# Decode step of two layers: in each pair's step the maximum's product and the exponential ahead of the preceding pair's value products; the kept pair's query product and output weights early

## The chip, the cores and the metric

One core of one Trainium2 chip. The metric is the device time of one launch in microseconds (us). The kernel before takes 515.19 us, the median of 3 runs (514.79 to 515.29). In the profiles PE is TensorE (matrix products), DVE VectorE, ACT ScalarE, POOL GpSimd, and SP the engine that issues the loads from HBM, the large memory, into SBUF, the core's own.

## The reference, cut to what matters

```python
x = x + A(layernorm(x)); x = x + B(layernorm(x))        # twice
def A(x, k_cache, v_cache, wq, wo):                     # B=Sq=1, D=640, 32 heads, Dh=192
    q = (x @ wq) per head
    k, v = the last W=4096 rows of the caches of each head
    p = softmax(q.k * Dh**-0.5);  o = p @ v
    return o.reshape(1, 1, 32*192) @ wo
def B(x, w_gate, w_up, w_down):                         # F=1536
    return (sigmoid(x @ w_gate) * (x @ w_up)) @ w_down
```

One token, bfloat16, the same weights and caches in both layers. In each layer every cache row is used for one product, so the work per byte is tiny. 219 MB pass from HBM into SBUF.

## The kernel before

The 32 heads go in 16 pairs. A pair has an A part (query weights and keys, 3.64 MB, in an A slot) and a B part (values and output weights, 3.64 MB, in a B slot). Layer one loads pair p's A part and pair p-1's B part in one transfer of 7.27 MB ("c" in `seq`, the order of the one DMA queue). A transfer is issued when both slots are free: `QK` frees an A slot, `PVn` (the output product) frees a B slot. Some pairs stay in SBUF for layer two; the "kept pair" PM = 1 keeps only its A part, and its output weights ("wom") are loaded over its query weights once its layer-two query product is done.

```python
    seq = [("a", 0, 0)] + [("c", 0, p) for p in range(1, 15)] + [("a", 0, 15), ("b", 0, 14)] + last_values(0, 15)
    seq += [("wol", 14), ("wol", 15)] + [(k,) for k in (*MW, *MV)] + [("a0", 0), ("a0", 1), ("a0", 2), ("a", 1, 3), ("b", 1, 2)]
    seq += [("wom",), ("b", 1, 3), ("a", 1, 4), ...]
    # [cut]
    def soft(x=0, hook=None, mid=None):
        # DVE: maximum of each score row
        pg.op("dve", lambda v: v.reduce_max(out=mx, in_=sc_x[0][:], axis=AX.X), ...)
        # ACT: diag = identity * maximum
        pg.op("act", lambda a: a.mul(out=diag[:], in_=ident, mul=mx), ...)
        if mid is not None:
            mid()
        # PE: the product that spreads the maximum over all partitions; DVE: two small ops make the bias
        pg.op("pe", lambda t: t.matmul(dmx[:, 0:P], lhsT=ones_f, rhs=diag[:], ...), ..., ex=[rb[2]])
        # [cut]
    def expo(x=0): ...   # ACT: e = exp(scores*s + bias), with its sum
    def ET(z): ...       # PE: 8 products transpose e; DVE copies it to et_sb
    def PVmm(p, z): ...  # PE: 32 value products; ACT: 2 evictions (o8_sb)
    def PVt(z): ...      # PE: RS, the sums' product (bank 4), and the transpose of o8; DVE: oTb = o * 1/sum
    def PVn(p, z): ...   # PE: 15 output products into yT, then release(slot of the values)

    def step(p, prev):
        if l == 0 and prev > 0:
            PVn(prev - 1, 1 - prev % 2)
        Q(p, 0)
        QK(p, 0)
        soft(0, mid=lambda: PVmm(prev, prev % 2))
        PVt(prev % 2)
        if l == 1:
            PVn(prev, prev % 2)
        expo()
        ET(p % 2)
```

Each engine runs its operations in program order, so the order of these calls is the order on PE, DVE and ACT. `step` runs 25 times: 15 in layer one, 10 in layer two.

## Time and profile before

| | |
|---|---|
| time | 515.19 us |
| busy | PE 49%, DVE 19%, ACT 17% |
| DMA | 218.97 MB, mean 426 GB/s; the main queue busy 99.2% of 16 engines' span |

The page of the kernel before; each digit after DMA is the busy share of a fortieth of the span in tenths, q1 is the main DMA queue with its share of 16 engines' span, and the last line is the chain of waits by engine:

```profile
span 513.6 us, 8566 instructions
DMA  9999999999999999999999999999999999999996
DMA packets 9676, 218.97 MB, mean 426 GB/s; under 512 B 1208, under 2 KB 1208, under 8 KB 4664
q1 hardware_dynamic: 9512, 218.63, 99.2%
DMA 66%; PE 22%; DVE 5%; ACT 3%; SPq 2%; issue 2%; DVEq 0%; POOL 0%; ACTq 0%; POOLq 0%
```

The queue has no hole of the size of a slice: DMA is the limit from end to end. The packets say it more sharply: a packet of 56,832 B takes 2,098 ns, which for 16 engines is 433 GB/s. The Trainium skill (DMA: Bandwidth & Descriptors, section "Where 436 GB/s comes from") gives 435.2 GB/s as the ceiling of the fabric; this trace agrees to 0.4%.

### The profile page before, as it was taken

The numbers are of one execution on the slowest core, as the hardware profiler recorded it, in microseconds if no ns is written. First come the engines' busy times: TensorE is split into PE (matmuls) and PEld (weight loads), VectorE is DVE, ScalarE is ACT, GpSimd is POOL, SyncE is SP. The second block draws the span as 40 slices with busy tenths as digits, with TensorE's granted clock in tenths as the row PEclk, the third lists the DMA queues.
The fourth block names the chain that finished last, engine by engine and source line by source line (L and its number), as shares of the span: only waits on it lengthen the run. The fifth ranks groups of instructions, "written<-read, shape, count | busy, mean of one in ns | idle before, by whom it ended". The sixth has DMA issues, their size and how long they took to land.

```text
span 513.6 us, 8566 instructions
## 1 busy us (share of the span) xinstructions
PE 250.7 (49%) x3716; PEld 136.8 (27%) x3716; DVE 97.8 (19%) x376; ACT 84.9 (17%) x171; POOL 4.3 (1%) x31
## 2 busy tenths in 40 slices
PE   0463255424543255325656767774535424543665
PEld 0231122112221122112325434442212112321234
DVE  0221212111210121112221333231212111210311
ACT  0110111011110111011121024130211011101220
POOL 0010000000000000000000000000000000000000
PEclk9965666566766666566665558686656566655765
DMA  9999999999999999999999999999999999999996
GB/s 425 429 422 425 426 431 438 456 434 425 429 425 434 430 438 451 438 429 425 410 417 408 407 440 429 424 432 429 446 430 447 434 443 429 425 430 423 423 429 286
DMA packets 9676, 218.97 MB, mean 426 GB/s; under 512 B 1208, under 2 KB 1208, under 8 KB 4664
## 3 DMA queue, kind: packets, MB, share of 16 engines
q1 hardware_dynamic: 9512, 218.63, 99.2%
q8 instruction: 13, 0.21, 0.1%
q10 hardware_dynamic: 144, 0.06, 0.0%
q14 instruction: 7, 0.06, 0.0%
HBM read 218.69 MB, written 0.00 MB: 426 GB/s over the span
## 4 chain that ended last, share of the span: by engine, by line
DMA 66%; PE 22%; DVE 5%; ACT 3%; SPq 2%; issue 2%; DVEq 0%; POOL 0%; ACTq 0%; POOLq 0%
DMA big<-in_uc_dram 57%; PE scores L409 8%; PE o L466 7%; DMA big<-in_wd_dram 6%; DMA big<-in_wu_dram 3%; ACT e_sb L433 3%; SPq L212 2%; PE bank L394 2%; PE bank L425 2%; PE bank L500 1%; DVE sc L426 1%; PE bank L439 1%; DVE qs L397 1%; DVE sc L419 1%; DVE sc L428 1%
## 5 line engine op out<-in xcount | busy, mean ns | idle before, releaser
L394 PE MATMUL bank<-sh,big 128*128 128x1 bf16 x480 | 17.7, 166 | 163.3 <-DMA big<-in_uc_dram 160.5
L409 PE MATMUL scores<-big,qs 128*32 128x512 bf16 x744 | 83.3, 617 | 10.3 <-DVE qs L397 10.3
L466 PE MATMUL o<-big,et_sb 128*2 128x384 bf16 x1024 | 76.8, 468 | 13.4 <-POOL sc L248 11.6
L422 ACT ACTIVATE diag<-cst,sc 128x128 f32<-128x128 bf16 x32 | 12.9, 402 | 326.7 <-PE o L466 210.6
L394 PEld LDWEIGHTS bank<-sh,big 128*128 128x128 bf16 x480 | 15.2, 104 | 167.4 <-issue 162.1
L419 DVE TENSOR_REDUCE sc<-scores 128x1 f32<-128x1024 f32 x31 | 37.9, 1223 | 78.9 <-PE scores L409 78.9
L466 PEld LDWEIGHTS o<-big,et_sb 128*2 128x2 bf16 x1024 | 32.1, 116 | 59.7 <-issue 39.8
L397 DVE TENSOR_TENSOR qs<-bank,cst 128x96 bf16<-128x96 f32 x32 | 8.2, 257 | 180.8 <-PE bank L394 180.8
L433 ACT ACTIVATE e_sb<-scores,sc 128x1024 bf16<-128x1024 f32 x31 | 37.3, 1204 | 20.3 <-DVE sc L428 18.0
L409 PEld LDWEIGHTS scores<-big,qs 128*32 128x32 bf16 x744 | 24.1, 134 | 44.6 <-issue 32.1
L473 ACT CAST o_sb<-o 128x384 bf16<-128x384 f32 x64 | 29.3, 472 | 25.9 <-PE o L466 25.5
L439 PE MATMUL bank<-cst,e_sb 128*128 128x8 bf16 x256 | 11.5, 168 | 25.6 <-ACT e_sb L433 25.4
L500 PE MATMUL bank<-sh,big 128*128 128x1 bf16 x480 | 17.0, 164 | 10.3 <-DVE sh L489 8.8
L426 DVE TENSOR_REDUCE sc<-bank 128x2 f32<-128x128 f32 x32 | 9.3, 292 | 60.3 <-PE bank L425 60.3
L425 PE MATMUL bank<-diag,sc 128*128 128x128 f32 x64 | 17.8, 364 | 4.8 <-ACT diag L422 4.6
L500 PEld LDWEIGHTS bank<-sh,big 128*128 128x128 bf16 x480 | 14.5, 98 | 12.9 <-DVE sh L489 8.8
L425 PEld LDWEIGHTS bank<-diag,sc 128*128 128x128 f32 x64 | 11.2, 219 | 19.7 <-ACT o_sb L473 9.6
L439 PEld LDWEIGHTS bank<-cst,e_sb 128*128 128x128 bf16 x256 | 8.7, 98 | 29.0 <-DVE sh L489 19.2
L443 DVE CAST et_sb<-bank 128x64 bf16<-128x64 f32 x32 | 7.2, 224 | 41.5 <-PE bank L439 41.5
L486 PE MATMUL bank<-cst,o_sb 128*128 128x1 bf16 x192 | 10.0, 167 | 7.0 <-DVE sc L426 6.2
L451 DVE RECIPROCAL sc<-o 64x1 f32<-64x1 f32 x64 | 10.5, 164 | 10.9 <-PE o L449 9.9
L449 PEld LDWEIGHTS o<-sc 128*128 128x128 f32 x64 | 10.7, 209 | 2.4 <-ACT o_sb L473 1.5
(70 smaller groups left out, 104.3 us busy)
## 6 DMA issues: line engine op xcount, KB each, us to landing
big<-in_uc_dram SPq DMA_DIRECT2D x20, 7104.0 KB, 24.6
big<-in_uc_dram SPq DMA_DIRECT2D x12, 3552.0 KB, 20.9
big<-in_uc_dram SPq DMA_DIRECT2D x1, 3072.0 KB, 22.8
big<-in_uc_dram SPq DMA_DIRECT2D x4, 768.0 KB, 13.6
big<-in_uc_dram SPq DMA_DIRECT2D x5, 480.0 KB, 13.5
big<-in_uc_dram SPq DMA_DIRECT2D x1, 2048.0 KB, 10.6
big<-in_uc_dram SPq DMA_DIRECT2D x1, 2016.0 KB, 13.0
big<-in_wg_dram SPq DMA_DIRECT2D x4, 480.0 KB, 15.8
```

The lines of the kernel that those rows point to most:

```text
L394: ins = t.matmul(qe[:, i:i + 1], lhsT=slot(sa, c * 2 * DH + c0, P), rhs=xq[:, c:c + 1], start=(c == 0), stop=(c == DC - 1))
L397: pg.op("dve", lambda v: v.tensor_tensor(out=qs[:, y], in0=qe[:, 0:3].unsqueeze(2).to_broadcast([P, 3, 32]), in1=mask3, op=ALU.mult), rd=[ ...
L409: ins = t.matmul(sc_x[1 + b][32 * j:32 * j + 32, :], lhsT=qs[:, y, k, :], rhs=slot(sa, WQE + k * W + (4 * b + j) * 512, 512), start=(k == ...
L419: pg.op("dve", lambda v: v.reduce_max(out=mx, in_=sc_x[0][:], axis=AX.X), wr=[res("mx")], ex=sc_x[3:5])
L422: pg.op("act", lambda a: a.mul(out=diag[:], in_=ident, mul=mx), rd=[res("cst"), res("mx")], wr=[res("diag")])
L425: pg.op("pe", lambda t: t.matmul(dmx[:, 0:P], lhsT=ones_f, rhs=diag[:], start=True, stop=True), rd=[res("diag"), res("ones")], ex=[rb[2]])
L426: pg.op("dve", lambda v: v.tensor_reduce(out=nb2, in_=dmx[:, 0:P].rearrange("p (a r) -> p r a", r=2), axis=AX.X, op=ALU.max, negate=True), ...
L433: pg.op("act", lambda a: a.activation(out=e_sb[:], in_=sc_x[0][:], func=ACT.Exp, bias=nbias, scale=srs_c, accum_out=rowsum), rd=[res("nbia ...
L439: ins = t.matmul(qe[:, 0:2 * NB].rearrange("p (r x) -> p r x", r=2)[:, :, 4 * b:4 * b + 4], lhsT=e_sb[:, b * P:(b + 1) * P], rhs=sel, star ...
L466: ins = t.matmul(o8[h][32 * j:32 * j + 2, 0:2 * DH].rearrange("p (a d) -> p a d", a=2), lhsT=et_sb[:, z, h * NB + 2 * u:h * NB + 2 * u + 2 ...
L473: pg.op("act", lambda a, h=h: a.copy(out=o8_sb[:, :, h * DH:(h + 1) * DH], in_=o8[h][:, 0:2 * DH].rearrange("p (a d) -> p a d", a=2)), wr= ...
L500: ins = t.matmul(yT[:, j:j + 1], lhsT=wo[:, c * D + j * P:c * D + (j + 1) * P], rhs=oTb[z][:, c:c + 1], start=False, stop=(c == 2), skip_g ...
```

## The change

Its intent: shorten the chain of a step (scores, maximum, spread product, exponential) by letting it no longer wait for the value products of the preceding pair; have the output weights of the kept pair in the queue earlier, where the queue is thin; and shorten the end of layer one. No byte and no operation goes away.

```diff
-    seq += [...] + [("a0", 0), ("a0", 1), ("a0", 2), ("a", 1, 3), ("b", 1, 2)]
-    seq += [("wom",), ("b", 1, 3), ...]
+    seq += [...] + [("a0", 0), ("wom",), ("a0", 1), ("a0", 2), ("a", 1, 3), ("b", 1, 2)]
+    seq += [("b", 1, 3), ...]
@@ step
             QK(p, 0)
-            soft(0, mid=lambda: PVmm(prev, prev % 2))
+            soft(0)
+            expo()
+            PVmm(prev, prev % 2)
+            ET(p % 2)
             PVt(prev % 2)
             if l == 1:
                 PVn(prev, prev % 2)
-            expo()
-            ET(p % 2)
@@ end of layer one (RS and Q get a parameter for their bank; PVt can leave RS out)
             PVmm(p, 1)
+            RS(1, 2)
             PVn(p - 1, 0)
-            PVt(1)
+            PVt(1, False)
             PVn(p, 1)
@@ layer two, start
             mark("a14_0", Q(14, 0))
+            mark("QM", Q(PM, 1, 5))
[cut]
             QK(0, 0)
-            mark("QM", Q(PM, 1))
             soft(0, mid=lambda: PVmm(14, 0))
```

More of the change, by code (lines that the diff above doesn't have):

```diff
@@ L227, in decode_kernel @@
     seq = [("a", 0, 0)] + [("c", 0, p) for p in range(1, 15)] + [("a", 0, 15), ("b", 0, 14)] + last_values(0, 15)
-    seq += [("wol", 14), ("wol", 15)] + [(k,) for k in (*MW, *MV)] + [("a0", 0), ("a0", 1), ("a0", 2), ("a", 1, 3), ("b", 1, 2)]
-    seq += [("wom",), ("b", 1, 3), ("a", 1, 4), ("b", 1, 4), ("a", 1, 5), ("a", 1, 6), ("b", 1, 5)]
+    seq += [("wol", 14), ("wol", 15)] + [(k,) for k in (*MW, *MV)] + [("a0", 0), ("wom",), ("a0", 1), ("a0", 2), ("a", 1, 3), ("b", 1, 2)]
+    seq += [("b", 1, 3), ("a", 1, 4), ("b", 1, 4), ("a", 1, 5), ("a", 1, 6), ("b", 1, 5)]
     seq += [("c", 1, p) for p in range(7, 13)] + [("a", 1, 13), ("b", 1, 12)] + last_values(1, 13)
@@ L386, in attention, with Q @@
         S = [(scores, bank[0], bank[1], rb[0], rb[1]), (o8_ps, bank[4], bank[5], rb[4], rb[5])]
-        def Q(p, y):
+        def Q(p, y, bk=2):
+            qe = bank[bk][:, 0:P]
             sa = A_SLOT[l][p]
@@ L395, in f @@
                 return ins
-            ev = pg.op("pe", f, rd=[res("xq"), rslot[sa]] + ([res("a00")] if l == 1 and p == 2 else []), ex=[rb[2]])
+            ev = pg.op("pe", f, rd=[res("xq"), rslot[sa]] + ([res("a00")] if l == 1 and p == 2 else []), ex=[rb[bk]])
             pg.op("dve", lambda v: v.tensor_tensor(out=qs[:, y], in0=qe[:, 0:3].unsqueeze(2).to_broadcast([P, 3, 32]), in1=mask3, op=ALU.mult),
-                  rd=[res("cst")], wr=[res(f"qs{y}")], ex=[rb[2]])
+                  rd=[res("cst")], wr=[res(f"qs{y}")], ex=[rb[bk]])
             return ev
@@ L445, in ET, with RS @@
                   rd=[res("rowsum"), res("wsel")], wr=[res(f"rs2{z}")])
-        def RS(z):
-            sm = bank[4][:, 2 * DH:2 * DH + 2]
-            pg.op("pe", lambda t: t.matmul(sm, lhsT=ones_f, rhs=rs2[z], start=True, stop=True), rd=[res(f"rs2{z}"), res("ones")], wr=[res("rsum")], ex=[rb[4]])
+        def RS(z, bk=4):
+            sm = bank[bk][:, 2 * DH:2 * DH + 2]
+            pg.op("pe", lambda t: t.matmul(sm, lhsT=ones_f, rhs=rs2[z], start=True, stop=True), rd=[res(f"rs2{z}"), res("ones")], wr=[res("rsum")], ex=[rb[bk]])
             for h in range(2):
-                rb[4].last["dve"] = pg.op("dve", lambda v, h=h: v.reciprocal(out=Rn[z][64 * h:64 * h + 64], in_=sm[64 * h:64 * h + 64, h:h + 1]),
+                rb[bk].last["dve"] = pg.op("dve", lambda v, h=h: v.reciprocal(out=Rn[z][64 * h:64 * h + 64], in_=sm[64 * h:64 * h + 64, h:h + 1]),
                                           rd=[res("rsum")], wr=[res(f"Rn{z}{h}")])
@@ L478, in PVout, with PVt @@
             PVn(p, z)
-        def PVt(z):
-            RS(z)
+        def PVt(z, sums=True):
+            if sums:
+                RS(z)
             def tm(t):
```

## The prediction

> **What bounds the kernel.** The DMA queue, from beginning to end. The profile page counts 218.97 MB at a mean 426 GB/s over 513.6 us; the queue of weights and caches is busy 99.2% of 16 engines' span, and all 40 slices but the last show DMA 9. PE has 49%. The chain of waits is 57% "DMA big<-in_uc_dram" and ends in the last down weights landing at 511.0 us, then a tail of 2.6 us. The Trainium skill (DMA: Bandwidth & Descriptors, "Where 436 GB/s comes from") puts the fabric's ceiling at 435 GB/s; the trace agrees to 2%.
>
> Compute counts only where a late release of a buffer lets the queue run dry. In the first layer's steps it does not: the load issued at 188.93 us (timeline) stands behind one that lands at 196.87 us. I worked out the backlog (bytes issued less bytes moved, at 0.43 MB/us) at every issue: 6 to 7 us in the first layer's steps, 8 us in the second's, over 10 us while layer two catches up (310 to 350 us). It is thin between 276 and 306 us, around the first MLP and the kept pairs: 2.3 us at 276.0, 2.7 us at 290.4, 4.2 us at 305.6.
>
> **What the change does.**
> 1. In each of 25 steps the product that spreads the maximum (0.49 us) no longer waits for the preceding pair's value products (2.1 to 2.7 us against maximum and diag, 1.23 + 0.40 us): 0.1 to 0.9 us off its start, and off the exponential's (1.40 us). But the value products start about 2.3 us after the scores instead of at once, and the transposed exponential follows them on PE: 4.3 to 5.0 us after the scores before, 4.5 to 5.1 us after (estimate). The two evictions (0.48 us each) stand behind the exponential on ACT, so the output product that frees a values buffer ends about 6.5 us after the scores; before, 5.2 to 5.8 us (layer one) and 4.6 us (layer two). Buffers come free 1 to 2 us later; the backlogs absorb it.
> 2. At the end of layer one the last step waits for values (landing 262.8 us). Its exponential now runs during that wait, so the last pair starts 2.5 us earlier, limited by last values and output weights landing: the MLP starts 0.5 to 1 us earlier. Backlog at 276 us: 2.3 to about 3 us.
> 3. The kept pair's query product (0.56 us) runs at the layer's start, so 0.49 MB of its output weights join the queue at about 290 us, not 306: 1.1 us more backlog where it was 2.7 us.
>
> No byte or operation is removed; the gains fall in shadow. Left over: packets of 3840 B take 149 ns in most windows, 154 to 162 ns between 275 and 295 us; all such excess adds up to some 0.5 us of queue time, of which more backlog may save part.
>
> **Prediction:** 514.9 us, 8 times in 10 between 514.1 and 515.7. Faster by over 2%: 0.01; within 2%: 0.98; slower: 0.01.
>
> **What would show it.** DMA digits and bytes unchanged; last weights landing at 511 us within 0.7. Loop issues 1 to 2 us later, landings unchanged. The first issue of a down weight moving from 276.0 to about 275.3.
>
> **What would make it wrong.** A dry queue that I don't see: layer two's catch-up steps lengthening by over 1 us each until a release comes after the backlog ends; or a changed packet rate.

## More of the kernel before

One step of layer one in the timeline. Columns: start us, duration us, engine, line, operation, out<-in, shapes, count, and in brackets how long the engine had been idle and what ended it. The MEMSET on POOL waits for a load and so marks its landing; the SPq line is the next load's issue:

```profile
213.63 0.09 POOL L248 MEMSET sc<- 1x1 f32 x1 [16.67 <-DMA big<-in_uc_dram]
214.56 2.75 PE L409 MATMUL scores<-big,qs 128*32 128x512 bf16 x24 [0.35 <-DVE qs L397]
217.09 2.35 PE L466 MATMUL o<-big,et_sb 128*2 128x384 bf16 x32
217.37 1.22 DVE L419 TENSOR_REDUCE sc<-scores 128x1 f32<-128x1024 f32 x1 [2.86 <-PE scores L409]
218.68 0.40 ACT L422 ACTIVATE diag<-cst,sc 128x128 f32<-128x128 bf16 x1 [13.86 <-PE o L466]
219.38 0.49 PE L425 MATMUL bank<-diag,sc 128*128 128x128 f32 x2
220.44 1.21 ACT L433 ACTIVATE e_sb<-scores,sc 128x1024 bf16<-128x1024 f32 x1 [0.45 <-DVE sc L428]
221.86 0.35 PE L439 MATMUL bank<-cst,e_sb 128*128 128x8 bf16 x8 [1.29 <-ACT e_sb L433]
222.07 0.52 PE L500 MATMUL bank<-sh,big 128*128 128x1 bf16 x15
222.67 0.33 SPq L212 DMA_DIRECT2D big<-in_uc_dram  x1
...
230.39 0.09 POOL L248 MEMSET sc<- 1x1 f32 x1 [16.67 <-DMA big<-in_uc_dram]
```

Three things to read. The value products (L466) fill PE while DVE takes the maximum; the spread product (L425) stands behind them. The work of a step ends 9 us after the landing and PE then waits for the next load, 16.75 us after the last. And the next load is issued at 222.67 us, while its predecessor lands at 230.39 us: **7.7 us of margin**. I use this margin (landing of the preceding load less the issue) throughout; over the ten loop issues of layer one its median is 7.6 us, over the four of layer two 8.7 us.

The granted clock of PE in that step (columns: stretch, length, busy us and instructions of PE, PEld, DVE, ACT, POOL, then granted clock, DMA share, GB/s):

```profile
217.30:219.40 2.10, 2.10 (x37) 0.79 (x25) 1.22 (x1) 0.72 (x2) 0.00 (x0) 0.62 1.00 433
219.40:220.00 0.60, 0.58 (x8) 0.50 (x4) 0.10 (x1) 0.53 (x2) 0.00 (x0) 1.00 1.97 852
```

After the value products PE's clock is at 1.00 when the spread product comes.

## The result

514.79 us, median of 4 runs (514.60 to 514.95), against 515.24 us for the kernel before in the same rounds (4 runs, 514.79 to 516.01). The ratio of the fast runs is 0.9989, 95% interval 0.9972 to 1.0007: the same. (A ratio is the mean time of one kernel's fast runs over that of the other's of the same rounds, so not quite the ratio of the medians.) Executions over 1.5% slower than the fastest of the same kernel are left out of the means.

The page of the changed kernel, the same lines:

```profile
span 513.6 us, 8573 instructions
DMA  9999999999999999999999999999999999999996
DMA packets 9676, 218.97 MB, mean 426 GB/s; under 512 B 1208, under 2 KB 1208, under 8 KB 4664
q1 hardware_dynamic: 9512, 218.63, 99.1%
DMA 63%; PE 24%; DVE 7%; ACT 2%; SPq 2%; issue 2%; DVEq 0%; POOL 0%; ACTq 0%; POOLq 0%
```

The DMA digits, packets and bytes are the same, and the last weights land at 511.0 us in both profiles, as forecast. The same step in the changed kernel (its lines lie 1 to 2 further down):

```profile
213.56 0.09 POOL L248 MEMSET sc<- 1x1 f32 x1 [16.83 <-DMA big<-in_uc_dram]
214.41 2.75 PE L410 MATMUL scores<-big,qs 128*32 128x512 bf16 x24 [0.35 <-DVE qs L398]
217.21 1.23 DVE L420 TENSOR_REDUCE sc<-scores 128x1 f32<-128x1024 f32 x1 [2.86 <-PE scores L410]
218.47 0.40 ACT L423 ACTIVATE diag<-cst,sc 128x128 f32<-128x128 bf16 x1 [12.47 <-DVE sc L420]
218.93 0.80 PE L426 MATMUL bank<-diag,sc 128*128 128x128 f32 x2 [1.76 <-ACT diag L423]
219.65 2.51 PE L467 MATMUL o<-big,et_sb 128*2 128x384 bf16 x32
220.29 1.21 ACT L434 ACTIVATE e_sb<-scores,sc 128x1024 bf16<-128x1024 f32 x1 [1.42 <-DVE sc L429]
222.10 0.35 PE L440 MATMUL bank<-cst,e_sb 128*128 128x8 bf16 x8
223.50 0.53 PE L502 MATMUL bank<-sh,big 128*128 128x1 bf16 x15 [0.36 <-DVE sh L491]
224.10 0.33 SPq L212 DMA_DIRECT2D big<-in_uc_dram  x1
...
230.29 0.09 POOL L248 MEMSET sc<- 1x1 f32 x1 [16.65 <-DMA big<-in_uc_dram]
```

The spread product comes earlier after the scores, as intended, but it takes 0.80 us, not 0.49. The exponential starts 3.13 us after the scores end (220.29 - 217.16); before, it was also 3.13 us (220.44 - 217.31). Over the eleven steps that I measured in layer one the median is 3.13 us after and 3.12 us before; the mean is 3.07 against 3.21 us, because the old order varies from 2.88 to 3.83 us and the new one only between 2.82 and 3.13 us. **The gain that the new order was made for is hardly there even inside the step:** 0.14 us in the mean. In this step PE has been idle for 1.76 us when the product comes, and the windows show the clock it then gets:

```profile
217.20:218.90 1.70, 0.00 (x0) 0.00 (x0) 1.23 (x1) 0.40 (x1) 0.00 (x0) 0.50 1.08 468
218.90:219.80 0.90, 0.87 (x6) 0.60 (x10) 0.04 (x1) 0.00 (x0) 0.00 (x0) 0.50 0.87 379
```

0.50 of the clock against 1.00 before. The value products that used to stand in the way had, by the clock records, also been what woke PE up. In both traces the clock changes on a fixed grid of 3.41 us, and each rise to 1.00 follows a stretch of the grid in which PE was busy for at least 2.7 us (not every such stretch is followed by a rise). With the value products PE works for nearly 6 us on end, from the query product at 213.65 us on; without them the query product and the scores give only 3.3 us of work in 3.7 us, and whether they fill a stretch depends on where the step falls on the grid. So in two of the eleven steps after the change (in three of `steps_only`'s) the product still got 1.00, took 0.49 us, and the exponential started at 2.82 us. No run put other work in that place, so the reason rests on these records. The Trainium skill (TensorE: Matmul & The Clock Gate, section "What's actually happening") states that the array runs at half its clock by default and that sustained activity of about 3.4 us releases it; this trace agrees on the two states (0.50 and 1.00) and shows their price on this product, 0.80 against 0.49 us. (Ends of matmuls are modelled in this profile; the start of the exponential, which is not, says the same.)

What did move is the release of the buffers, to the worse. The output product ends 7.2 us after the scores in layer one and 7.1 us in layer two (medians); before, 5.5 us in layer one and 4.3 us in layer two. The issue at 224.10 us has 6.2 us of margin. Medians:

| | margin, layer one | margin, layer two | landing interval, layer one (mean) |
|---|---|---|---|
| before | 7.6 us | 8.7 us | 16.75 us |
| after | 5.9 us | 5.9 us | 16.76 us |

The loads still land every 16.75 us.

### The profile page after: what moved, and what is told of

The parts are those of the page before. It is cut to its first block, busy times and chain, and to the rows that moved or that the text cites. A ratio compares the mean times of both kernels' runs of the same rounds, so it can differ in the third digit from the quotient of the medians.

```text
span 513.6 us, 8573 instructions
## 1 busy us (share of the span) xinstructions
PE 263.4 (51%) x3716; PEld 137.6 (27%) x3716; DVE 99.2 (19%) x376; ACT 85.2 (17%) x171; POOL 4.2 (1%) x31
## 3 DMA queue, kind: packets, MB, share of 16 engines
HBM read 218.69 MB, written 0.00 MB: 426 GB/s over the span
## 4 chain that ended last, share of the span: by engine, by line
DMA 63%; PE 24%; DVE 7%; ACT 2%; SPq 2%; issue 2%; DVEq 0%; POOL 0%; ACTq 0%; POOLq 0%
DMA big<-in_uc_dram 54%; PE scores L410 8%; PE o L467 7%; DMA big<-in_wd_dram 6%; DVE sc L420 3%; DMA big<-in_wu_dram 3%; PE bank L426 2%; SPq L212 2%; PE bank L395 2%; PE bank L502 1%; ACT e_sb L434 1%; PE bank L440 1%; ACT diag L423 1%; DVE sc L452 1%; DVE qs L398 1%
## 5 line engine op out<-in xcount | busy, mean ns | idle before, releaser
L410 PE MATMUL scores<-big,qs 128*32 128x512 bf16 x744 | 81.5, 605 | 9.9 <-DVE qs L398 9.9
L467 PE MATMUL o<-big,et_sb 128*2 128x384 bf16 x1024 | 78.7, 474 | 5.9 <-DMA big<-in_uc_dram 3.4
L426 PE MATMUL bank<-diag,sc 128*128 128x128 f32 x64 | 22.5, 447 | 47.9 <-ACT diag L423 47.9
L467 PEld LDWEIGHTS o<-big,et_sb 128*2 128x2 bf16 x1024 | 28.0, 108 | 43.8 <-issue 31.1
L426 PEld LDWEIGHTS bank<-diag,sc 128*128 128x128 f32 x64 | 14.1, 274 | 73.0 <-ACT diag L423 71.5
L450 PE MATMUL o<-sc 128*128 128x2 f32 x62 | 14.0, 295 | 0.6 <-ACT o_sb L474 0.6
L450 PEld LDWEIGHTS o<-sc 128*128 128x128 f32 x62 | 12.1, 243 | 1.9 <-ACT o_sb L474 1.3
```

What stands on the lines that cost most here:

```text
L410: ins = t.matmul(sc_x[1 + b][32 * j:32 * j + 32, :], lhsT=qs[:, y, k, :], rhs=slot(sa, WQE + k * W + (4 * b + j) * 512, 512), start=(k == ...
L450: pg.op("pe", lambda t: t.matmul(sm, lhsT=ones_f, rhs=rs2[z], start=True, stop=True), rd=[res(f"rs2{z}"), res("ones")], wr=[res("rsum")], ...
L467: ins = t.matmul(o8[h][32 * j:32 * j + 2, 0:2 * DH].rearrange("p (a d) -> p a d", a=2), lhsT=et_sb[:, z, h * NB + 2 * u:h * NB + 2 * u + 2 ...
```

## The experiments

Twelve kernels ran. The first three were run with 9 runs of the kernel before on the same chip; each group below has its own runs of before.

### The parts alone, and the changed kernel again

`steps_only` is the kernel before with the new body of `step` and nothing else:

```diff
-            soft(0, mid=lambda: PVmm(prev, prev % 2))
+            soft(0)
+            expo()
+            PVmm(prev, prev % 2)
+            ET(p % 2)
             PVt(prev % 2)
             if l == 1:
                 PVn(prev, prev % 2)
-            expo()
-            ET(p % 2)
```

> The kernel before with the new order inside the 25 steps and nothing else of the change. Shadow theory (the DMA queue never runs dry, so no order of the compute is seen): within 0.2% of before, ratio 0.998 to 1.002; loop issues as late as in the changed kernel (some 7.3 us after the scores end, before 5.2 to 5.8), last weight packet at 510.6 us within 0.3. Rival (the parts of the change cancel: the steps lose, the kept pair's early query product gains): 0.3% or more slower, ratio above 1.003.

Measured: 514.93 us median of 5 (514.69 to 515.81), ratio 0.9999, interval 0.9986 to 1.0013. Margins 6.0 and 5.8 us. The new order alone costs no time and gains none.

`kept_only` is the changed kernel with the old body of `step` and the old end of layer one; what is left is the early `Q(PM, 1, 5)` and the early `("wom",)`:

```diff
             mark("a14_0", Q(14, 0))
+            mark("QM", Q(PM, 1, 5))
@@ seq
-    ("a0", 0), ("a0", 1), ("a0", 2), ("a", 1, 3), ("b", 1, 2), ("wom",), ...
+    ("a0", 0), ("wom",), ("a0", 1), ("a0", 2), ("a", 1, 3), ("b", 1, 2), ...
```

> The kernel before with the early query product and early output weights of the kept pair, the steps in the old order. Shadow theory: within 0.2% of before, ratio 0.998 to 1.002; backlog at 290 us some 0.5 to 1 us larger. Rival (parts cancel): 0.3% or more faster, ratio below 0.997. If packets of 3840 B between 275 and 290 us drop from 154-162 to 149 ns only because of the earlier end of layer one, this run does not show that drop, and steps_only does.

Measured: 514.96 us median of 5 (514.66 to 515.15), ratio 0.9993, interval 0.9979 to 1.0007. Margins as in the kernel before (7.5 and 8.7 us); the backlog at 290.4 us is 3.5 us against 2.7. The rival that the parts cancel each other by 0.3% or more is out: by the intervals neither moves the time by more than about 0.2%.

On the packets of 3,840 B: between 275 and 280 us they average 149.0 ns here and 150.7 ns in `steps_only`, against 161.7 ns in the profile of before. So neither part is the reason: the slow packets come and go from profile to profile. `thin_before` (below), whose code is that of the kernel before up to 289 us, has 149.8 ns there, and between 280 and 290 us `after_again` has 161.9 ns.

`after_again` is the changed kernel unaltered, as a control.

> The changed kernel again, as a control on the same chip: ratio 0.998 to 1.001. Both theories say the same.

Measured: 514.95 us median of 5 (514.59 to 516.82), ratio 0.9990, interval 0.9977 to 1.0004. The profiled run was the odd one, 516.82 us: between 284 and 290 us, in the first MLP, its DMA moved 318 GB/s where the first profile of the changed kernel moved 423, which alone is some 1.5 us (estimate, 6 us at these rates) of the 1.9 us by which its span is longer. Runs of the kernel before reach 516.41 us too, so a run as long as this is not particular to the change. What disturbs the thin place in such a run, and whether it is the same in the runs of the kernel before, is not settled.

### Where the load is not the limit

`light_before` and `light_after` are the two kernels with a quarter of each double load from pair 4 of layer one on, and in layer two. The rest of the buffer keeps older data, so the results are wrong by design, while the number of operations is unchanged:

```diff
-            pg.dma(q_dma(slot(first, 0, 2 * UNIT), uc[p]), ...)
+            n_in = UNIT // 2 if l == 1 or p >= 4 else 2 * UNIT
+            pg.dma(q_dma(slot(first, 0, n_in), uc[p][:, 0:n_in]), ...)
```

> The kernel before with a quarter of the bytes in the 12 double loads of layer one from pair 4 (11 of them) and in the 6 of layer two; wrong results on purpose (old data is used). DMA is then no longer the limit in these steps; the step's own chain is. From the trace of before a step's chain is 8.6 to 9.4 us where layer two catches up, against 16.75 us of load: about 8 us less in each of some 17 steps, 385 us, between 370 and 400. If compute already bound the steps, the time would stay above 480.

> The changed kernel with the same quarter loads. Shadow theory with a longer chain: in the changed order PE waits out the maximum and the diag (1.23 + 0.40 us) before the value products, so a step's chain is some 11 us: 405 to 420 us, 5 to 9% slower than light_before. Rival (the change shortens the step, as its intent says, and DMA only hides the gain): faster than light_before, by 0.5 us or more in each of 17 steps, 2% or more.

Measured: `light_before` 376.82 us median of 5 (374.52 to 380.84, of which 380.84 is a slow run and left out of the ratio), ratio to before 0.7273; `light_after` 395.74 us (392.15 to 396.25), ratio 0.7679. The changed kernel is 5.6% slower (0.7679 over 0.7273). The absolute value for `light_after` was missed, 396 against 405 to 420 expected, because I had put its step at 11 us. The start of the query product in successive steps gives the period; first `light_before`, then `light_after`:

```profile
107.68 0.53 PE L395 MATMUL bank<-sh,big 128*128 128x1 bf16 x15
...
116.29 0.53 PE L395 MATMUL bank<-sh,big 128*128 128x1 bf16 x15
```

```profile
102.43 0.51 PE L396 MATMUL bank<-sh,big 128*128 128x1 bf16 x15
...
112.41 0.51 PE L396 MATMUL bank<-sh,big 128*128 128x1 bf16 x15
```

8.6 us in the old order and 10.0 us in the new for these two; over the twelve steps from 62.7 us on the mean is 9.0 and 9.9 us. And who waits for whom between 90 and 180 us, first `light_before`, then `light_after` (engine, line and what it waited for: us in total, times, longest):

```profile
PE bank L440 <- ACT e_sb L434: 11.6, 9, 1.3
```

```profile
PE bank L427 <- ACT diag L424: 15.8, 9, 1.8
```

In the new order PE stands idle for 1.8 us in each of nine steps while the maximum and the diag are made; in `light_before` the value products fill that time. The old order has a wait of its own, 1.3 us for the exponential, which the new order fills: it exchanges one wait for a longer one. So the reason for the missing gain is not only that DMA hides it. The rival, that the change shortens the step and DMA merely hides it, is refuted: where compute is the limit, the new order is the slower one.

### How much slack the steps have

The next kernels delay the output product that frees a values buffer in layer one's loop (14 steps) by n chained copies on ACT, results unchanged:

```diff
             if l == 0 and prev > 0:
-                PVn(prev - 1, 1 - prev % 2)
+                for i in range(n):
+                    pg.op("act", lambda a: a.copy(out=diag[:], in_=ident),
+                          rd=[res("cst"), res("diag") if i else res(f"oTb{1 - prev % 2}")], wr=[res("diag")])
+                PVn(prev - 1, 1 - prev % 2, [res("diag")])     # waits for the last copy
```

`held5_after` (n = 5) and `held12_after` (n = 12) are built on the changed kernel, `held12_before` (n = 12) on the kernel before.

> The changed kernel with 5 chained copies on ACT (0.40 us each and a wait, some 2.3 us together) ahead of each output product that frees a values buffer in layer one's loop (14 steps). Backlog theory: the issue comes 2.3 us later, the backlog at it falls from 4.4-5.6 us to 2.1-3.3 us, the queue does not run dry: same time within 0.3%. Rival (steps have no slack left, the compute chain counts): 14 x 2.3 = 32 us or 6% more.

> The same with 12 copies, some 5.3 us. Backlog theory: the issue comes after the backlog of 4.4-5.6 us and the first-byte time is not covered, so the queue runs dry for some 0.5 to 1.5 us in each step: 5 to 20 us more, 1 to 4%. Rival: 14 x 5.3 = 74 us more, or nothing.

> The kernel before with the same 12 copies, 5.3 us. Its backlog at the issue is 6.5-7 us, and ACT starts the copies while the sums are still under way, so the issue comes about 4.7 us later: the queue stays fed or nearly so, within 0.5% of before. If held12_after is slower by 1% or more and this one is not, the change has spent some 2 us of the slack that the kernel before had.

Twelve copies took 3.9 us, not 5.3 (0.33 us each), five took 1.6 us. The kernel before ran in 515.39 us beside them (median of 7). Margins and landing intervals are those of the same ten loop issues of layer one:

| | time | ratio, interval | margin, median | landing interval, mean |
|---|---|---|---|---|
| held5_after | 519.35 us | 1.0079, 1.0048 to 1.0110 | 4.2 us | 16.89 us |
| held12_before | 519.03 us | 1.0095, 1.0056 to 1.0133 | 4.3 us | 17.02 us |
| held12_after | 535.32 us | 1.0370, 1.0333 to 1.0408 | 3.1 us | 18.32 us |

The same 3.9 us of delay costs 20 us on the changed kernel and 4 us on the kernel before. (Of the 4 us of `held5_after`, 2.3 us have been lost when the last load of the loop lands in its profile, at 249.2 us against 246.9 us in the changed kernel; the rest goes after it.) Two of my three expectations were too mild: `held5_after` should have cost nothing and `held12_before` under 0.5%. I had taken the queue to be fed as long as the backlog is above zero. The table says otherwise: a median margin of 4.2 us already costs. In `held12_after` the margins run from 1.7 to 6.2 us: its three loads with 1.7 to 1.9 us landed 3.2 to 3.7 us late, those with 4.7 us and more at most 0.3 us late. Its trace shows why. First the timeline, an issue with 1.7 us of margin and the landing of that load 20.3 us after its predecessor's instead of 16.75:

```profile
187.93 37.56 SPq L212 DMA_DIRECT2D big<-in_uc_dram  x3
189.61 0.09 POOL L248 MEMSET sc<- 1x1 f32 x1 [16.75 <-DMA big<-in_uc_dram]
...
210.00 0.09 POOL L248 MEMSET sc<- 1x1 f32 x1 [20.30 <-DMA big<-in_uc_dram]
```

(The duration in the SPq line spans three merged issues.) Then the windows; the last two columns count the packets by their start:

```profile
185.00:186.00 1.00, 0.00 (x0) 0.00 (x0) 0.00 (x0) 0.91 (x4) 0.00 (x0) 0.50 0.26 114
186.00:187.00 1.00, 0.00 (x0) 0.00 (x0) 0.00 (x0) 0.91 (x4) 0.00 (x0) 0.50 0.01 0
187.00:188.00 1.00, 0.56 (x15) 0.48 (x15) 0.00 (x0) 0.07 (x1) 0.00 (x0) 0.50 0.13 57
188.00:189.00 1.00, 0.00 (x0) 0.00 (x0) 0.00 (x0) 0.00 (x0) 0.00 (x0) 0.50 1.76 511
```

From 186 us on hardly a packet starts, although the preceding load lands only at 189.6 us: the load lands when the last of its 16 engines is done. In the packets' records 16 packets of 4 bytes close the load, taken here as one for each engine: fifteen end between 186.5 and 187.9 us, the last at 189.2 us. The new load's first packets start at 188.9 us, 1.0 us after its issue, and take 2.6 to 3.6 us instead of 2.1. So here the issue would have had to come about 4 us (3 us from the first engine's end to the landing and 1 us of start) ahead of the landing for no engine to run dry. That is an estimate from this one hole. In layer one of the kernels before and after the same closing packets lie 1.6 to 1.9 us apart, so that some 3 us would do there (estimate); why 4.2 us still costs 0.1 to 0.3 us a load is thus not fully explained. What is measured: 5.7 us and more cost nothing that can be told from the noise. The changed kernel, at 5.9 us, has some 1.5 us of real slack left where the kernel before had over 3 (estimate, the margins less the 4.2 us that cost).

### The thin place

`thin_before` and `thin_kept` hold up the first score products of layer two by the same 12 copies, in the kernel before and in `kept_only`, where the backlog is smallest:

```diff
+            for i in range(12):
+                pg.op("act", lambda a: a.copy(out=diag[:], in_=ident),
+                      rd=[res("cst"), res("diag") if i else res("qs0")], wr=[res("diag")])
-            mark("a14_1", QK(14, 0, ks=(0,)))
+            mark("a14_1", QK(14, 0, ks=(0,), more=[res("diag")]))
```

> The kernel before with 12 chained copies on ACT (3.9 us, as measured in held12_after) between the second layer's first query product and its first score products, where the backlog is thinnest (2.7 us at 290.4 us). The issues of the kept pair's buffers come 3.9 us later and the queue runs dry there once: 2 to 4 us more than before, ratio 1.004 to 1.008. If the thin place has more slack than the backlog says, within 0.5 us.

> kept_only with the same 12 copies at the same place. The kept pair's output weights (0.49 MB, 1.1 us of queue time) are already in the queue when the wait begins, so the queue is dry for some 1 us less: 0.5 to 1.5 us faster than thin_before. If the early output weights are worth nothing even in a queue that runs dry, the two are equal within 0.3 us, by the times of their landings.

Measured, beside 515.28 us of before (9 runs): `thin_before` 518.28 us (517.85 to 518.91), ratio 1.0056, interval 1.0042 to 1.0070; `thin_kept` 517.41 us (517.31 to 517.82), ratio 1.0040, interval 1.0027 to 1.0054. The ranges of the two do not overlap, though the intervals of their ratios do. The windows show the hole, `thin_before` and then `thin_kept`:

```profile
292.00:294.00 2.00, 0.84 (x12) 0.32 (x16) 0.00 (x0) 1.01 (x4) 0.00 (x0) 0.50 0.39 159
294.00:296.00 2.00, 2.00 (x26) 0.64 (x19) 0.00 (x0) 0.00 (x0) 0.00 (x0) 0.50 0.51 82
```

```profile
292.00:294.00 2.00, 0.74 (x8) 0.30 (x12) 0.00 (x0) 1.11 (x4) 0.00 (x0) 0.50 0.89 342
294.00:296.00 2.00, 2.00 (x22) 0.55 (x15) 0.00 (x0) 0.00 (x0) 0.00 (x0) 0.50 0.53 117
```

342 against 159 GB/s in the first stretch: the early output weights fill part of the hole, and in the traces the 130th megabyte lands 0.9 us earlier. So the early kept pair is worth about 0.9 us, but only when the queue runs dry there, and undisturbed it does not.

### Keeping one half of the change

`kept_and_sums` is the changed kernel with the old body of `step`; the early kept pair and the sums' other bank stay. `held12_mix` is that with the 12 copies ahead of each freeing output product.

```diff
@@ step, against the changed kernel
-            soft(0)
-            expo()
-            PVmm(prev, prev % 2)
-            ET(p % 2)
+            soft(0, mid=lambda: PVmm(prev, prev % 2))
             PVt(prev % 2)
             if l == 1:
                 PVn(prev, prev % 2)
+            expo()
+            ET(p % 2)
```

> The changed kernel with the old order inside the steps: it keeps what made the thin places thicker (early query product and output weights, the sums' other bank) and gives back the 1 to 2 us of slack in the steps. By the shadow theory no faster than before or after where nothing disturbs: ratio to before 0.998 to 1.001; backlog at the loop's issues 6.5 to 7 us again, first issue of a down weight at about 275.

> kept_and_sums with the same 12 copies ahead of each freeing output product of layer one. If the slack that the new step order spends is what made held12_after slow, this run is like held12_before: 517.5 to 519.5 us, ratio 1.004 to 1.010, not 535 us. If the early parts of the change had anything to do with it, it is above 522 us.

Measured: `kept_and_sums` 514.75 us median of 5 (514.64 to 514.98), ratio 0.9987, interval 0.9973 to 1.0001, margins 7.5 and 8.5 us. It is no faster than before or after, as expected. Its first issue of a down weight came at 275.89 us, not at about 275, so that part of the expectation was wrong: with the old order the sums' other bank alone does not bring the MLP forward. `held12_mix` 520.49 us median of 4 (519.52 to 520.69), ratio 1.0101, interval 1.0083 to 1.0120. That is a little above the stated range (517.5 to 519.5 us), but like `held12_before` (1.0095) and far from `held12_after` (1.0370). It is thus the order in the step, not the rest of the change, that spent the slack. No version here beats both kernels; the bytes and the packets are the same in all of them.

## Why the prediction was right

**The bound and the time: right.** 514.79 us against 514.9 forecast, in the range. The reason held: no byte goes away and the queue never runs dry, so nothing else is seen. The parts alone (0.9999 and 0.9993) and the control (0.9990) leave no room for a hidden trade between them of more than about 0.2%.

**Step 1, the spread product and the exponential: wrong in what it gains.** The prediction had "0.1 to 0.9 us off its start, and off the exponential's". The product's start did move forward (1.76 us after the scores against a mean of 2.12 us); of the exponential's, 0.14 us of the mean is left and nothing of the median (3.13 against 3.12 us). The term that failed is the 0.49 us of the product itself, taken from a trace in which PE was awake: it became 0.80 us at a granted clock of 0.50 in nine of the eleven steps.

**Step 1, the later release: right in direction, too small.** "About 6.5 us after the scores" was 7.2 us; the same clock explains part of it (value products 2.5 to 2.7 us, spread product 0.80 us). "1 to 2 us later" was 1.7 us of margin in layer one and 2.8 us in layer two. "The backlogs absorb it" was right, but with less to spare than the text implied: it treated any backlog above zero as enough, and in the held kernels a margin of 4.2 us already cost time.

**Step 2, the end of layer one: the mechanism is there, the number is in part luck.** The last pair's value products start at 266.5 us against 269.0 before, 2.4 us earlier (forecast 2.5), and then wait for its values to land, as forecast. The first down weight is issued at 274.95 us against 276.02 before, forecast "about 275.3". But the parts alone gave 275.53 (`steps_only`), 275.46 (`kept_only`, which does not touch this place) and 275.89 us (`kept_and_sums`), and `thin_before`, whose code up to here is that of the kernel before, gave 275.42 us. Profiles of the same code thus differ by 0.6 us, and I cannot assign the 1.1 us to the parts.

**Step 3, the kept pair: right as to the mechanism, too large in size.** Its output weights were issued at 289.31 us. The backlog at the next issue was 3.0 us against 2.7, not 1.1 us more; in `kept_only`, with nothing else changed, 3.5 us. That it pays once the queue runs dry was shown by the thin pair.

**The leftover of 0.5 us from small packets** was not to be resolved: the difference of before and after lies within the interval, and the slower packets of the first trace come and go whatever the kernel.

## What to carry to other kernels

When a queue is full from end to end, a reordering of compute cannot be judged by the time; take the load away (as in the light pair) to see whether the order is good, and add a delay (as in the held kernels) to see what slack it spends. Work that stands in front of a critical operation may be the filler that keeps PE busy and its clock up: cost the operation at the clock it will get after the move, not at the one it had. The margin of a prefetch is not its backlog: it must cover the spread between DMA engines at the end of the preceding load and the start of the new one.

## What the Trainium skill lacked or had wrong

- DMA: Bandwidth & Descriptors, "Where 436 GB/s comes from", says in its warning that for HBM to SBUF the HBM side (about 358 GB/s) binds. Here one core alone read 218.69 MB from HBM at a mean 426 GB/s, and its large packets ran at 433 GB/s over 16 engines. The page's own note on single-core numbers fits; that sentence needs "with both cores streaming".
- The same page, "Latency and other measured facts", gives a first-byte time of about 0.6 us and a fixed cost of about 2 us. In the hole of `held12_after` the first packets start 1.0 us after the issue begins and 0.6 us after it ends. The page lacks how early a prefetch must be issued behind another: for loads of 7.27 MB a margin of 5.7 us cost nothing measurable, a median of 4.2 us cost 0.1 to 0.3 us a load, and 1.7 to 1.9 us cost 3.2 to 3.7 us; single engines finish up to 3 us before the load lands.
- TensorE: Matmul & The Clock Gate, "What's actually happening": the two states are as stated (0.50 and 1.00 granted). The page lacks the warning that moving filler work away from in front of a short fp32 product can cost what the move gains (0.80 against 0.49 us here).
